# Two unused tiles that move the operands of the MoE matmuls to multiples of 512 bytes

## The chip, the cores and the metric

The kernel runs on one core of a Trainium2 chip. The metric is the device time of one execution in microseconds (us), as the median of three runs. Differences of about 0.2% are the least that a measurement of this kernel can tell from no change.

## What is computed

The reference chains three parts. The first is a retention-style attention over 4 batches, 8 heads, 576 positions and 64 features per head: scores are multiplied by a decay matrix (no softmax) and by the values. The second and third are feed-forward layers on the 2304 resulting tokens of 512 features: one with 2048 hidden units and a squared ReLU, and one with four experts of 1024 hidden units each, weighted by given probabilities.

```python
ret = scale * (q @ k.T) * Dmat            # Dmat[i, j] = gamma ** (i - j) for i >= j
x = (ret @ v) as [2304, 512]
x = square(relu(x @ w_in)) @ w_out        # 512 -> 2048 -> 512
p = probs / probs.sum(-1)
out = sum over e of p[:, e] * (relu(x @ w1[e]) @ w2[e])   # 4 x (512 -> 1024 -> 512)
```

## The kernel before, in words

**Numbers in two parts.** Each operand of a feed-forward matmul is kept as a pair of fp32r tiles, a rounded high part and the rest: `xh` and `xl` for tokens, `whi` and `wlo` for weights, `ghi` and `glo` for the hidden layer. A product is made of three matmuls: high by high, low by high, high by low.

**Stages.** The attention comes first, in its own pools, which are closed at its end; `finish` (L281) writes its result to `xh` and `xl`. Then comes what is called the MoE part here: a loop over 24 weight chunks c (8 of the first feed-forward layer, then 4 for each of the 4 experts), each of 256 hidden units (f = 0, 1 of 128 each), and inside it over five token groups g of 512, 512, 512, 512 and 256 tokens. For each (c, g), `layer1` (L356) runs, and after it the second layer of the pair before, `layer2_1` (L381) for c < 8 and `layer2_2` (L405) for c >= 8.

**Matmuls.** TensorE executes a matmul as a weight load of the stationary operand (128 columns here) and a stream of the moving operand.
- L365, `layer1`: stationary a slice of `whi` or `wlo`, moving a slice of `xh` or `xl`; 12 for each of two PSUM tiles.
- L389, `layer2_1`: stationary a slice of `whi` or `wlo`, moving `ghi` or `glo`; 6 for each of four PSUM tiles.
- L418, `layer2_2`: the other way round, stationary a slice of `ghi` or `glo`, moving a half of `whi` or `wlo`; 6 for each of g's 128-token blocks.

In all there are 4800 matmuls that stream 512 columns (2304 at L365, 768 at L389, 1728 at L418) and 768 that stream 256 (576 and 192, of the fifth group).

**Other engines.** ScalarE and VectorE empty the PSUM tiles (L369 to L376, L395 to L401, L424 to L428), GpSimd makes low parts (L122, L372, L401), and `split_w` (L101) converts the next chunk's weights while this one is used. The order on each engine is the order of the program.

**Where tiles lie.** Pools take space in each partition in the order in which they are opened, and a tile's size is rounded up to 32 bytes. The first free byte is 16512. `const` (L35) holds no tile in the kernel before. In the compiled program of before the tiles that MoE matmuls read begin at these bytes:

```
tile        bytes      begins at                 over a multiple of 512
xh, xl      36864      16512, 53376              128, 128
whi (2)      8192      123008, 131200            128, 128
wlo (2)      8192      139392, 147584            128, 128
pr, prsum   288, 72    192640, 192928            (not read by matmuls)
ghi (3)      4096      193024, 197120, 201216    0, 0, 0
glo (3)      4096      205312, 209408, 213504    0, 0, 0
```

All slices of them that a matmul reads begin a multiple of 512 bytes after the tile's start (128 columns of fp32r are 512 bytes, 512 columns 2048, a row of `xh` 9216), so each slice stands over a multiple of 512 as its tile does.

Of the kernel before, what the change touches and what calls it, by code (L numbers as in the profile page):

```python
# [6 lines left out]
F32 = mybir.dt.float32  # L7
# [25 lines left out]
def tile_kernel(ctx, tc, qT, kT, kn, vn, v4d, mask, qdec, kdec, wd, w, probs, out):  # L33
    nc = tc.nc
    const = ctx.enter_context(tc.tile_pool(name="const", bufs=1))  # L35
    xp = ctx.enter_context(tc.tile_pool(name="xp", bufs=1))
    wrp = ctx.enter_context(tc.tile_pool(name="wrp", bufs=4))
    cvp = ctx.enter_context(tc.tile_pool(name="cvp", bufs=1))
# [297 lines left out]
    with tc.manual_schedule():  # L336
# [4 lines left out]
        yp = ctx.enter_context(tc.tile_pool(name="yp", bufs=1))  # L341
# [3 lines left out]
        yacc = [yp.tile([128, KT, GS[g]], F32, name=f"y{g}", tag=f"acc{g}") for g in range(NG)]  # L345
        pr = yp.tile([128, NTT, 4], F32, name="pr")
        psum_ = yp.tile([128, NTT], F32, name="prsum")
        nc.sync.dma_start(out=pr, in_=probs)
        nc.vector.tensor_reduce(out=psum_, in_=pr, axis=mybir.AxisListType.X, op=ALU.add)
        nc.vector.tensor_scalar_add(psum_, psum_, 1e-9)  # L350
# [157 lines left out]
```

## Time and profile before

| | us |
|---|---|
| median of 3 runs | 1288.08 (1287.55 to 1289.81) |
| the profiled execution, its own time | 1288.76 |
| its span, first to last instruction | 1286.5 |
| PE (matmul) busy | 1272.8, 99% |
| PEld (weight load) busy | 1059.2, 82% |
| VectorE, GpSimd, ScalarE busy | 658.7, 332.9, 299.0 |

PE is TensorE's matmul stream, PEld its weight loads, which run beside it. The profile's duration of a matmul reaches into the next one, since matmuls are pipelined; what a matmul costs in a dense stream is the distance from its start to the next one's, called its pitch here. A row of the timeline gives the start in us, the duration, engine, line, and the tile written and the tiles read, the moving operand's high or low part and the stationary one's in the order of the profile's own names. A row of a group gives the number of instructions, their summed busy time in us, the mean of one in ns and the idle time before them.

### The profile page before, as it was taken

How to read it: one execution, taken by the hardware profiler on the slowest of the kernel's cores; microseconds unless marked ns; L12 is line 12 of the kernel's file. 1: busy time of each engine (PE TensorE's matmuls, PEld its weight loads, DVE VectorE, ACT ScalarE, POOL GpSimd, SP SyncE). 2: the span in 40 equal slices, each digit the busy share in tenths (PEclk: the TensorE clock that was granted, in tenths of full speed). 3: DMA queues.
4: the chain of work that ended last, by engine and by line, in shares of the span. 5: the costliest groups of instructions: out<-in, count | busy, mean ns of one | idle time of the engine just before them, and what ended most of it. 6: DMA issues, size and time to landing. Idle time of an engine off the chain costs nothing.

```text
span 1286.5 us, 16159 instructions
## 1 busy us (share of the span) xinstructions
PE 1272.8 (99%) x6720; PEld 1059.2 (82%) x6720; DVE 658.7 (51%) x946; ACT 299.0 (23%) x636; POOL 332.9 (26%) x270
## 2 busy tenths in 40 slices
PE   7999999999999999999999999999999999999998
PEld 6878888888888888888888888888888888888887
DVE  4965777887877851143343433434434433434334
ACT  3544322223222253311111111111111111111110
POOL 4654454444444592011010010110110110110100
PEclk9999999999999999999999999999999999999999
DMA  9931110111110000000000000000000000000003
GB/s 330 327 105 34 38 61 23 44 50 33 49 47 28 25 33 25 9 33 24 10 33 11 22 33 9 25 29 12 25 25 9 34 25 9 33 17 17 1 34 114
DMA packets 27465, 59.42 MB, mean 46 GB/s; under 512 B 3328, under 2 KB 4352, under 8 KB 27392
## 3 DMA queue, kind: packets, MB, share of 16 engines
q1 hardware_dynamic: 26880, 57.69, 13.1%
q8 instruction: 52, 0.85, 0.3%
q10 hardware_dynamic: 512, 0.70, 0.2%
q14 instruction: 21, 0.17, 0.0%
HBM read 53.66 MB, written 4.72 MB: 45 GB/s over the span
## 4 chain that ended last, share of the span: by engine, by line
PE 97%; DVE 1%; DMA 1%; ACT 0%; issue 0%; ACTq 0%; DVEq 0%
PE h L365 46%; PE o L418 31%; PE o L389 16%; PE xo L264 1%; PE qk L212 1%; PE xo L276 1%; PE state L240 1%; DMA v_n<-vn 1%; DMA k_n<-kn 0%; DVE cv_e L82 0%; DVE cv_p L86 0%; DVE xl L290 0%; ACT xh L289 0%; DVE pt L228 0%; DVE cv_m L88 0%; DVE cv_e L84 0%
## 5 line engine op out<-in xcount | busy, mean ns | idle before, releaser
L365 PE MATMUL h<-xh,whi 128*128 128x512 f32 (+1 forms) x960 | 353.7, 368 | 0.8 <-DVE xl L290 0.8
L365 PE MATMUL h<-xh,wlo 128*128 128x512 f32 (+1 forms) x960 | 354.2, 369 | 0.0
L365 PE MATMUL h<-xl,whi 128*128 128x512 f32 (+1 forms) x960 | 353.3, 368 | 0.0
L375 DVE SCALAR_TENSOR_TENSOR glo<-h,ghi 128x512 fp32r<-128x512 f32 (+1 forms) x160 | 102.2, 638 | 354.7 <-ACT ghi L374 354.7
L426 DVE SCALAR_TENSOR_TENSOR oacc<-o,pr,oacc 128x512 f32<-128x512 f32 x270 | 202.6, 750 | 139.4 <-PE o L418 135.1
L122 POOL TENSOR_TENSOR wlo<-wraw,whi 128x512 fp32r<-128x512 f32 x64 | 82.7, 1293 | 645.7 <-ACT whi L121 616.5
L374 ACT ACTIVATE ghi<-h 128x512 fp32r<-128x512 f32 (+1 forms) x160 | 89.0, 556 | 644.0 <-PE h L365 644.0
L418 PE MATMUL o<-whi,ghi 128*128 128x512 f32 x576 | 227.8, 395 | 0.0
L418 PE MATMUL o<-wlo,ghi 128*128 128x512 f32 x576 | 227.4, 395 | 0.0
L418 PE MATMUL o<-whi,glo 128*128 128x512 f32 x576 | 227.3, 395 | 0.0
L365 PEld LDWEIGHTS h<-xh,whi 128*128 128x128 f32 x960 | 180.8, 188 | 32.7 <-DVE xl L290 1.0
L365 PEld LDWEIGHTS h<-xl,whi 128*128 128x128 f32 x960 | 180.7, 188 | 32.2
L365 PEld LDWEIGHTS h<-xh,wlo 128*128 128x128 f32 x960 | 180.7, 188 | 30.9
L372 POOL TENSOR_TENSOR glo<-r,ghi 128x512 fp32r<-128x512 f32 (+1 forms) x80 | 95.8, 1199 | 142.6 <-ACT ghi L371 142.6
L370 DVE TENSOR_TENSOR r<-r 128x512 f32<-128x512 f32 (+1 forms) x80 | 81.4, 1017 | 94.9 <-ACT r L369 94.9
L418 PEld LDWEIGHTS o<-wlo,ghi 128*128 128x128 f32 x576 | 108.5, 188 | 25.7
L418 PEld LDWEIGHTS o<-whi,glo 128*128 128x128 f32 x576 | 108.7, 189 | 24.6
L418 PEld LDWEIGHTS o<-whi,ghi 128*128 128x128 f32 x576 | 108.5, 188 | 24.3
L389 PE MATMUL o<-ghi,wlo 128*128 128x512 f32 (+1 forms) x320 | 119.4, 373 | 0.0
L389 PE MATMUL o<-glo,whi 128*128 128x512 f32 (+1 forms) x320 | 119.1, 372 | 0.0
L389 PE MATMUL o<-ghi,whi 128*128 128x512 f32 (+1 forms) x320 | 119.0, 372 | 0.0
L397 DVE TENSOR_TENSOR y<-o,y 128x512 f32<-128x512 f32 (+1 forms) x140 | 85.5, 627 | 8.1 <-PE o L389 7.4
(51 smaller groups left out, 937.6 us busy)
## 6 DMA issues: line engine op xcount, KB each, us to landing
wraw<-wd SPq DMA_DIRECT2D x32, 512.0 KB, 3.6
wraw<-w SPq DMA_DIRECT2D x64, 256.0 KB, 2.7
q_t<-qT SPq DMA_DIRECT2D x16, 288.0 KB, 5.2
out<-oacc SPq DMA_DIRECT2D x18, 256.0 KB, 2.0
kt<-kT SPq DMA_DIRECT2D x15, 288.0 KB, 5.4
v_n<-vn SPq DMA_DIRECT2D x16, 256.0 KB, 4.8
k_n<-kn SPq DMA_DIRECT2D x15, 256.0 KB, 5.4
qd<-qdec SPq DMA_DIRECT2D x4, 224.0 KB, 5.0
```

Of the source, the lines that this page charges most:

```text
L122: nc.gpsimd.tensor_tensor(out=lo[:, s], in0=r, in1=f32(hi[:, s]), op=ALU.subtract)
L212: nc.tensor.matmul(qk[:, j, w : w + m], k_t[p, o : o + C], q_t[p, o : o + m], start=True, stop=True, skip_group_check=True,)
L240: nc.tensor.matmul(st[64 * j : 64 * j + 64, :], k_n[:, c, j, :], v_n[:, c, j, :], start=(c == 0), stop=(c == 3), skip_group_check=True,)
L365: nc.tensor.matmul(h, a[:, f, k, :], x[:, k, :], start=(n == 0), stop=(n == 3 * KT - 1))
L370: nc.vector.tensor_tensor(out=r, in0=r, in1=r, op=ALU.mult)
L372: nc.gpsimd.tensor_tensor(out=lo[:, f, :], in0=r, in1=f32(hi[:, f, :]), op=ALU.subtract)
L374: nc.scalar.activation(out=hi[:, f, :], in_=h, func=ACTF.Relu)
L375: nc.vector.scalar_tensor_tensor(out=lo[:, f, :], in0=h, scalar=0.0, in1=f32(hi[:, f, :]), op0=ALU.max, op1=ALU.subtract)
L389: nc.tensor.matmul(o, a[:, f, 128 * m : 128 * m + 128], x[:, f, :], start=(n == 0), stop=(n == 3 * FT - 1))
L397: nc.vector.tensor_tensor(out=y, in0=o, in1=y, op=ALU.add)
L418: nc.tensor.matmul(o, a[:, f, 128 * m : 128 * m + 128], x[:, f, :], start=(n == 0), stop=(n == 3 * FT - 1))
L426: nc.vector.scalar_tensor_tensor(out=acc, in0=o, scalar=pr[:, tt, e : e + 1], in1=acc, op0=ALU.mult, op1=ALU.add)
```

## The change

Two tiles are asked for and never written or read.

```diff
     const = ctx.enter_context(tc.tile_pool(name="const", bufs=1))
+
+    const.tile([128, 480], F32, name="pad0")
     xp = ctx.enter_context(tc.tile_pool(name="xp", bufs=1))
...
         psum_ = yp.tile([128, NTT], F32, name="prsum")
+        yp.tile([128, 32], F32, name="pad1")
         nc.sync.dma_start(out=pr, in_=probs)
```

`pad0` is 1920 bytes in each partition ahead of all other pools, and `pad1` is 128 bytes in `yp`, ahead of the pools of `ghi`, `glo` and `r`. By the sizes above, every tile from `xh` on begins 1920 bytes later, and `ghi`, `glo` and `r` 2048 bytes later: `xh` at 18432, `xl` at 55296, `whi` at 124928 and 133120, `wlo` at 141312 and 149504, the first `ghi` at 195072, the first `glo` at 207360. All of these are multiples of 512. The attention's tiles all move by the same 1920 bytes. No instruction is added, removed or reordered.

## Rows read from the trace of the kernel before

**Rows 1.** The profile's page, busy time of PE, and granted clock in 40 slices.
```profile
PE 1272.8 (99%) x6720; PEld 1059.2 (82%) x6720; DVE 658.7 (51%) x946; ACT 299.0 (23%) x636; POOL 332.9 (26%) x270
...
PEclk9999999999999999999999999999999999999999
```

**Rows 2.** The page's chain that ended last, by engine and by line.
```profile
PE 97%; DVE 1%; DMA 1%; ACT 0%; issue 0%; ACTq 0%; DVEq 0%
PE h L365 46%; PE o L418 31%; PE o L389 16%; PE xo L264 1%; PE qk L212 1%; PE xo L276 1%; PE state L240 1%; DMA v_n<-vn 1%; DMA k_n<-kn 0%; DVE cv_e L82 0%; DVE cv_p L86 0%; DVE xl L290 0%; ACT xh L289 0%; DVE pt L228 0%; DVE cv_m L88 0%; DVE cv_e L84 0%
```

**Rows 3.** Busy time by stage: stretch, its us, engines' busy (count), clock, DMA.
```profile
0.00:85.00 85.00, 74.91 (x1153) 65.35 (x1153) 59.79 (x96) 40.08 (x166) 47.97 (x50) 1.00 0.83 288
85.00:480.00 395.00, 395.00 (x1888) 329.97 (x1889) 291.22 (x414) 123.55 (x225) 199.52 (x153) 1.00 0.12 38
480.00:1283.00 803.00, 802.85 (x3681) 663.90 (x3680) 307.03 (x437) 135.33 (x245) 85.41 (x68) 1.00 0.07 24
```

**Rows 4.** Timeline of PE: the MoE part's first and last matmul.
```profile
84.91 0.50 PE L365 MATMUL h<-xh,whi 128*128 128x512 f32 x1 [0.84 <-DVE xl L290]
...
1282.46 0.40 PE L418 MATMUL o<-wlo,ghi 128*128 128x512 f32 x1
```

**Rows 5.** Groups of matmuls by line and shape, whole span, one row of three.
```profile
L365 PE MATMUL h<-xh,wlo 128*128 128x512 f32 x768 | 300.0, 391 | 0.0
...
L418 PE MATMUL o<-whi,ghi 128*128 128x512 f32 x576 | 227.8, 395 | 0.0
...
L389 PE MATMUL o<-ghi,wlo 128*128 128x512 f32 x256 | 101.2, 395 | 0.0
...
L365 PE MATMUL h<-xh,wlo 128*128 128x256 f32 x192 | 54.2, 282 | 0.0
```

**Rows 6.** Timeline, PE and PEld, second half of an L365 block, then L389.
```profile
215.27 0.39 PE L365 MATMUL h<-xh,whi 128*128 128x512 f32 x1
...
217.76 0.39 PE L365 MATMUL h<-xh,wlo 128*128 128x512 f32 x1
217.77 0.19 PEld L389 LDWEIGHTS o<-ghi,whi 128*128 128x128 f32 x1
217.99 0.40 PE L389 MATMUL o<-ghi,whi 128*128 128x512 f32 x1
...
223.58 0.28 PE L365 MATMUL h<-xh,whi 128*128 128x256 f32 x1
```

**Rows 7.** Timeline, PE and PEld, one L365 block and the L418 block behind it.
```profile
700.84 0.39 PE L365 MATMUL h<-xh,whi 128*128 128x512 f32 x1
...
706.07 0.40 PE L365 MATMUL h<-xh,wlo 128*128 128x512 f32 x1
706.07 0.19 PEld L418 LDWEIGHTS o<-whi,ghi 128*128 128x128 f32 x1
...
706.30 0.40 PE L418 MATMUL o<-whi,ghi 128*128 128x512 f32 x1
...
711.65 0.40 PE L418 MATMUL o<-wlo,ghi 128*128 128x512 f32 x1
711.89 0.39 PE L365 MATMUL h<-xh,whi 128*128 128x512 f32 x1
```

**Rows 8.** Group of one: the last L365 matmul ahead of L389 (at 217.76).
```profile
L365 PE MATMUL h<-xh,wlo 128*128 128x512 f32 x1 | 0.4, 389 | 0.0
```

**Rows 9.** Group of one: the last L365 matmul ahead of L418 (at 706.07).
```profile
L365 PE MATMUL h<-xh,wlo 128*128 128x512 f32 x1 | 0.4, 396 | 0.0
```

**Rows 10.** Timeline of PE: twelve 256-column matmuls, then L418.
```profile
724.35 0.28 PE L365 MATMUL h<-xh,whi 128*128 128x256 f32 x1
...
725.79 0.39 PE L418 MATMUL o<-whi,ghi 128*128 128x512 f32 x1
```

**Rows 11.** Groups of VectorE and GpSimd that follow each PSUM tile.
```profile
L426 DVE SCALAR_TENSOR_TENSOR oacc<-o,pr,oacc 128x512 f32<-128x512 f32 x270 | 202.6, 750 | 139.4 <-PE o L418 135.1
...
L372 POOL TENSOR_TENSOR glo<-r,ghi 128x512 fp32r<-128x512 f32 (+1 forms) x80 | 95.8, 1199 | 142.6 <-ACT ghi L371 142.6
```

## The prediction

> **What bounds the kernel now.** I read the page's first lines, then the chain of work that ended last, then busy time by stage. [...] By stage, the attention takes the first 85 us; from there to 1283 us PE has no gap worth naming (395.00 busy of 395, 802.85 of 803) [rows 3]. So nothing that waits, loads or copies can give time back in the MoE part. Only the pitch of the matmuls can.
>
> The MoE part runs from 84.91 to 1282.46 us plus its last matmul's pitch of 0.23 [rows 4], 1197.8 us in all, for 4800 matmuls of 512 columns and 768 of 256.
>
> **The pitch is not one number.** In the rows by shape a 512-column matmul has a mean duration of 391 ns at L365 (390 in its two rows that are not shown) but 395 ns at L418 and at L389 (394 in one row not shown) [rows 5]. The durations reach into the next matmul, so I take pitches from the timeline. The second half of an L365 block goes from 215.27 to 217.99, twelve matmuls in 2.72 us: 226.7 ns each. The L389 block behind it goes from 217.99 to 223.58, 24 matmuls in 5.59 us: 232.9 ns [rows 6]. An L418 block goes from 706.30 to 711.89, again 24 in 5.59: 232.9 ns [rows 7]. Duration less pitch is 162 ns in both cases (389 less 226.7, 395 less 232.9) [rows 5, 6, 8], so differences of mean durations are differences of pitch.
>
> Three things could tell the slow lines from the fast one: the length of the group that shares a PSUM tile (6 against 12), the code, and the addresses. The border between blocks separates them. While a matmul streams, PEld loads the stationary operand of the next one: both start within 0.01 us [rows 6, 7]. The last L365 matmul ahead of an L389 block streams `xh` (128 bytes over a multiple of 512) beside a load of `whi` (also 128): 389 ns [rows 8]. The same instruction ahead of an L418 block streams `xh` (128) beside a load of `ghi` (0): 396 ns [rows 9]. It is the same line, group length, position and moving tile; only the operand that is loaded meanwhile differs. So I take it that the pair read at one time sets the pitch: both at the same distance from a multiple of 512 is fast, 128 bytes apart is slow. L389 streams 0 beside loads of 128, L418 streams 128 beside loads of 0, and both show 232.9. Multiples of 512 beyond that don't count: L365 reads weight slices at eight of them, and the second half of the block at 215.27 keeps 226.7 through four.
>
> One border doesn't fit at once: the last L418 matmul, at 711.65, streams `whi`'s twin `wlo` (128) beside a load of `whi` (128), and its pitch is still 0.24 [rows 7]. And an L365 block behind an L418 block takes 5.46 us, 227.5 ns each (700.84 to 706.30), against 226.7 in a settled half [rows 6, 7]. I read both as time to settle after a slow block: L365's mean of 390.3 (391, 390 and 390 in its three rows) lies 1.3 above the 389 of a settled one [rows 5, 8]. After the change no pair differs, so nothing is left to settle from.
>
> **The change part by part.**
>
> *pad0* moves the attention, `xh`, `xl`, `whi` and `wlo` by 1920 bytes, which is 384 over a multiple of 512; *pad1* moves `ghi` and `glo` by 128 more. No instruction, semaphore or DMA is added, and an unused tile has no reader to wait for. What it costs is space: the highest tile, the third `r`, ends 2048 bytes higher. Afterwards all MoE operands stand at 0 over a multiple of 512, so each pair is equal, as at L365 now.
>
> - L418: 1728 matmuls from 395 to 389 ns: 1728 x 6 = 10.4 us less [rows 5, 8].
> - L389: 768 of 512 columns from 394.7 (mean of the three rows) to 389: 4.4 us less.
> - L365: 2304 of 512 columns from 390.3 (mean of the three) to 389: 3.0 us less.
> - 256 columns: twelve from 724.35 to 725.79 are 120.0 ns each in a settled half [rows 10], and the mean of 282 less 162 is 120 too [rows 5]. Nothing here.
>
> Sum: 10.4 + 4.4 + 3.0 = 17.8 us. The other way round, free of the rounding of means to 1 ns: 4800 x 0.2267 + 768 x 0.120 = 1180.3 us in place of 1197.8 [rows 4, 6, 10], 17.5 less. I take 17.5.
>
> All of it is on the path, as PE is what ends the stage. What would be late next is far off: VectorE's step for an L418 tile takes 750 ns where the tile's six matmuls will take 1360, with 135 us idle in wait for PE, and GpSimd's 1199 ns at L372 stands beside twelve matmuls of 2720 ns [rows 11].
>
> *The attention* moves as a whole, so no distance between two of its tiles changes. Its 85 us have loads and engines interleaved (PE 74.91 of 85 busy) [rows 3]. If distance alone counts it costs nothing. The trace has no row at the new positions; the nearest price is 7 ns (396 less 389) [rows 8, 9] for each of its 1152 matmuls either way, 8 us if all were bound by their streams. I take 0, since their starts hang on other engines too, and keep 1 us either way for the range.
>
> [...]
>
> **The rivals.**
>
> *No change.* The two sorts of matmul differ for another reason that goes with the tile (its place in the partition, or that it was written shortly before), and moving all by a few hundred bytes alters nothing; or the unused tiles take no space. For it: the border shows which tile, not which address bit. Against it: `ghi` and `glo` lie in six places over 24 KB and `whi` and `wlo` in four, and L389 and L418 swap their roles at the same pitch [rows 6, 7]. Time 1288.
>
> *Slower: an operand at a multiple of 512 is what costs.* The slow pairs are just those with one operand at 0; the fast ones have none. No pair of the trace has both at 0, and after the change every one has. If it costs 6 ns for each such operand, L365 pays 2 x 6 above 389 (10.7 above its mean; 2304 x 10.7 = 24.7 us) and the 2496 others 6 more than now (15.0): 1288.1 + 39.7 = 1328. If the second costs nothing, only L365 loses, 4.7 x 2304 = 10.8: 1299. It decides from the first L365 block on. [...]
>
> *More than forecast: the constant goes too.* From 256 to 512 columns the settled pitch grows by 106.7 ns (226.7 less 120.0) [rows 6, 10], that is 2.4 columns a ns; so both carry a constant of 13.3 ns. If that were a matter of position too, 5568 x 13.3 = 74 us more would go: 1196.5. Against it: it is the same at both widths and at every slice. [...]
>
> *Half.* L389 or L418 settles at a pitch of its own between the two: 8 us less, 1280.
>
> **How the numbers follow.** Forecast 0.70: 1288.1 - 17.5 = 1270.6, within 2 us either way. The profiled execution, 1288.76 for a span of 1286.5, should come to a span near 1269.0, and its time lies 0.7 above the median. Half 0.06, no change 0.11, slower 0.09, more 0.04. The range must take in no change to leave out less than 2 in 10: 1267 to 1290, which holds 0.87. A measurement tells about 0.2%, 2.6 us, from no change: faster 0.80 (forecast, half, more), same 0.11, slower 0.09.
>
> **What would show it.** Right: mean durations of 389 ns in all nine 512-column groups; blocks of 24 at L389 and L418 in 5.44 us; no settling at the start of an L365 block. Wrong: 395 at L418 and L389 as before (no change); L365 above 391 (slower); anything under 385 (more). The prediction falls if the position of each operand counts for itself and not the distance of the two.

## The result

The changed kernel takes 1271.7 us (median of four runs, 1271.3 to 1272.47) against 1288.6 us for the kernel before, run beside it: a ratio of 0.987, 95% interval 0.985 to 0.989. The forecast was 1270.6 us. The profiled execution has a span of 1269.1 us (forecast 1269.0) and a time of 1271.3.

The page of the changed kernel, busy time and the chain that ended last. TensorE is as full as before and the chain lies where it did [rows 1, 2], and its granted clock is 1.00 in both stages, as the rows by stage below show.

```profile
PE 1254.8 (99%) x6720; PEld 1057.3 (83%) x6720; DVE 650.4 (51%) x946; ACT 298.7 (24%) x636; POOL 334.2 (26%) x270
...
PEclk9999999999999999999999999999999999999999
...
PE 97%; DVE 2%; DMA 0%; ACT 0%; issue 0%; ACTq 0%; DVEq 0%
```

Matmuls of the changed kernel by line and shape (L368, L421 and L392 are L365, L418 and L389 of before; columns as in [rows 5]).

```profile
L368 PE MATMUL h<-xh,whi 128*128 128x512 f32 x768 | 299.0, 389 | 0.8 <-DVE xl L292 0.8
...
L368 PE MATMUL h<-xh,wlo 128*128 128x512 f32 x768 | 298.8, 389 | 0.0
L421 PE MATMUL o<-whi,ghi 128*128 128x512 f32 x576 | 224.3, 389 | 0.0
...
L421 PE MATMUL o<-wlo,ghi 128*128 128x512 f32 x576 | 224.1, 389 | 0.0
L392 PE MATMUL o<-ghi,whi 128*128 128x512 f32 x256 | 99.7, 389 | 0.0
...
L392 PE MATMUL o<-ghi,wlo 128*128 128x512 f32 x256 | 99.6, 389 | 0.0
L368 PE MATMUL h<-xh,wlo 128*128 128x256 f32 x192 | 54.3, 283 | 0.0
```

All nine groups of 512 columns stand at 389 ns, where the kernel before had 394 to 395 at L418 and L389 and 390 to 391 at L365 [rows 5]. The groups of 256 columns moved by 1 ns at most.

Timeline of PE in the changed kernel: one L392 block (start to start, 24 matmuls), and the first half of the next one, which follows matmuls of 256 columns.

```profile
215.77 0.39 PE L392 MATMUL o<-ghi,whi 128*128 128x512 f32 x1
...
221.21 0.28 PE L368 MATMUL h<-xh,whi 128*128 128x256 f32 x1
...
224.08 0.40 PE L392 MATMUL o<-ghi,whi 128*128 128x512 f32 x1
...
226.83 0.39 PE L392 MATMUL o<-ghi,whi 128*128 128x512 f32 x1
```

The first block takes 5.44 us, 226.7 ns for each matmul, where its like took 5.59 before [rows 6]. The first half of the next takes 2.75 us for twelve, 229.2 ns each: behind 256-column matmuls there is still a short settling.

Busy time by stage of the changed kernel (columns as in [rows 3]), cut at the MoE part's first matmul and behind its last one.

```profile
0.00:84.36 84.36, 73.67 (x1152) 64.42 (x1153) 60.02 (x96) 40.00 (x166) 48.66 (x50) 1.00 0.83 290
84.36:1265.29 1180.93, 1180.93 (x5568) 992.87 (x5568) 589.65 (x849) 258.72 (x470) 285.56 (x220) 1.00 0.09 29
```

The MoE part takes 1180.9 us in place of 1197.8, 16.9 less. It starts 0.55 earlier [rows 4], which is the rest of the 17.4 by which the span fell; the tail behind it is 3.8 us in both.

### The profile page after: what moved, and what is told of

Same layout as the page of the kernel before. It is cut to its first block, busy times and chain, and to the rows that moved or that the text cites. A ratio compares the mean times of both kernels' runs of the same rounds, so it can differ in the third digit from the quotient of the medians.

```text
span 1269.1 us, 16159 instructions
## 1 busy us (share of the span) xinstructions
PE 1254.8 (99%) x6720; PEld 1057.3 (83%) x6720; DVE 650.4 (51%) x946; ACT 298.7 (24%) x636; POOL 334.2 (26%) x270
## 4 chain that ended last, share of the span: by engine, by line
PE 97%; DVE 2%; DMA 0%; ACT 0%; issue 0%; ACTq 0%; DVEq 0%
PE h L368 47%; PE o L421 31%; PE o L392 16%; PE xo L266 1%; PE qk L214 1%; PE xo L278 1%; PE state L242 1%; DMA k_n<-kn 0%; DVE cv_e L84 0%; DVE xl L292 0%; DVE cv_e L86 0%; DVE pt L230 0%; ACT xh L291 0%; DVE pt L228 0%; DVE cv_e L82 0%
## 5 line engine op out<-in xcount | busy, mean ns | idle before, releaser
L368 PE MATMUL h<-xh,whi 128*128 128x512 f32 (+1 forms) x960 | 353.2, 368 | 0.8 <-DVE xl L292 0.8
L368 PE MATMUL h<-xl,whi 128*128 128x512 f32 (+1 forms) x960 | 353.2, 368 | 0.0
L368 PE MATMUL h<-xh,wlo 128*128 128x512 f32 (+1 forms) x960 | 353.1, 368 | 0.0
L421 PE MATMUL o<-whi,ghi 128*128 128x512 f32 x576 | 224.3, 389 | 0.0
L421 PE MATMUL o<-whi,glo 128*128 128x512 f32 x576 | 224.3, 389 | 0.0
L421 PE MATMUL o<-wlo,ghi 128*128 128x512 f32 x576 | 224.1, 389 | 0.0
L368 PEld LDWEIGHTS h<-xh,whi 128*128 128x128 f32 x960 | 181.0, 189 | 31.7 <-DVE xl L292 1.0
L368 PEld LDWEIGHTS h<-xl,whi 128*128 128x128 f32 x960 | 180.9, 188 | 30.5
L368 PEld LDWEIGHTS h<-xh,wlo 128*128 128x128 f32 x960 | 180.9, 188 | 30.0
L373 DVE TENSOR_TENSOR r<-r 128x512 f32<-128x512 f32 (+1 forms) x80 | 78.4, 981 | 95.8 <-ACT r L372 95.8
L421 PEld LDWEIGHTS o<-wlo,ghi 128*128 128x128 f32 x576 | 108.1, 188 | 22.6
L421 PEld LDWEIGHTS o<-whi,ghi 128*128 128x128 f32 x576 | 108.2, 188 | 22.1
L421 PEld LDWEIGHTS o<-whi,glo 128*128 128x128 f32 x576 | 108.2, 188 | 21.8
L392 PE MATMUL o<-glo,whi 128*128 128x512 f32 (+1 forms) x320 | 117.8, 368 | 0.0
L392 PE MATMUL o<-ghi,whi 128*128 128x512 f32 (+1 forms) x320 | 117.8, 368 | 0.0
L392 PE MATMUL o<-ghi,wlo 128*128 128x512 f32 (+1 forms) x320 | 117.7, 368 | 0.0
```

The source lines that it names most:

```text
L368: nc.tensor.matmul(h, a[:, f, k, :], x[:, k, :], start=(n == 0), stop=(n == 3 * KT - 1))
L373: nc.vector.tensor_tensor(out=r, in0=r, in1=r, op=ALU.mult)
L392: nc.tensor.matmul(o, a[:, f, 128 * m : 128 * m + 128], x[:, f, :], start=(n == 0), stop=(n == 3 * FT - 1))
L421: nc.tensor.matmul(o, a[:, f, 128 * m : 128 * m + 128], x[:, f, :], start=(n == 0), stop=(n == 3 * FT - 1))
```

## The experiments

Every experiment starts from the kernel before and only moves tiles, so the same instructions run on the same numbers. "Place" is a tile's start over a multiple of 512 bytes, the "load" is that of a matmul's stationary operand, and the "stream" is its moving operand. A time without a range is that of one execution, and the time in brackets behind it is the kernel before on the same chip. The lines added move L365, L389 and L418 down by one to three.

### Each unused tile alone

```diff
         psum_ = yp.tile([128, NTT], F32, name="prsum")
+        yp.tile([128, 32], F32, name="pad1")
```

> Only pad1 is added: xh, xl, whi, wlo stay 128 bytes over a multiple of 512, and ghi, glo go from 0 to 128. Distance theory (only the distance of the two operands read at one time counts): all pairs equal, every 512-column group at 389 ns, time as of the changed kernel, 1271.7 within 2 us. Position theory (an operand gains by standing at a multiple of 512): no operand stands there any more, so no gain, 1288 or more. Attention unmoved, so it stays at the 84.9 us of before.

Measured: 1271.7 us (1271.1 to 1272.2) against 1289.3, ratio 0.986, interval 0.985 to 0.988. By line and shape:

```profile
L366 PE MATMUL h<-xh,whi 128*128 128x512 f32 x768 | 299.0, 389 | 0.8 <-DVE xl L290 0.8
...
L419 PE MATMUL o<-whi,ghi 128*128 128x512 f32 x576 | 224.3, 389 | 0.0
...
L390 PE MATMUL o<-ghi,whi 128*128 128x512 f32 x256 | 99.7, 389 | 0.0
```

The same busy times to 0.1 us as in the changed kernel, with no operand at a multiple of 512. 128 bytes in one place are the whole gain.

```diff
     const = ctx.enter_context(tc.tile_pool(name="const", bufs=1))
+    const.tile([128, 480], F32, name="pad0")
```

> Only pad0 is added: xh, xl, whi, wlo at 0, ghi and glo at 384 over a multiple of 512, so the pairs of L365 are equal as before and those of L389 and L418 are still 128 bytes apart (384 against 0). Distance theory: as before, L389 and L418 at 395 ns, 1288 within 2 us, less up to 0.6 us for the attention. Position theory: L365 and half the operands of the other two stand at multiples of 512, so some part of the gain, 1276 to 1283.

Measured: 1288.5 us (before: 1289.3). By line and shape:

```profile
L366 PE MATMUL h<-xh,wlo 128*128 128x512 f32 x768 | 300.0, 391 | 0.0
...
L419 PE MATMUL o<-whi,ghi 128*128 128x512 f32 x576 | 227.8, 395 | 0.0
...
L390 PE MATMUL o<-ghi,wlo 128*128 128x512 f32 x256 | 101.2, 395 | 0.0
```

Each of these three rows equals that of before to the tenth of a microsecond [rows 5]. A shift of all tiles alike does nothing to the MoE part, although it puts `xh`, `xl`, `whi` and `wlo` at multiples of 512.

### Equal places that are a multiple of nothing larger than 32

```diff
+    const.tile([128, 8], F32, name="pad0")
...
+        yp.tile([128, 32], F32, name="pad1")
```

> A pad of 32 bytes ahead of all tiles and one of 128 ahead of ghi and glo: all operands at 160 over a multiple of 512, equal, but at no multiple of 64. Distance theory: 389 ns in every 512-column group, 1271.5 within 2 us. If equal operands must also stand at a multiple of 64 or 128 bytes: above 389 ns in all three lines, 1275 or more.

Measured: 1271.3 us (before: 1290.2), all nine groups of 512 columns at 389 ns. So the single operand needs no alignment beyond 32 bytes here.

### The lines change places

```diff
+    wpad = ctx.enter_context(tc.tile_pool(name="wpad", bufs=1))
+    wpad.tile([128, 32], F32, name="padw")
     wp = ctx.enter_context(tc.tile_pool(name="wp", bufs=2))
...
+        yp.tile([128, 32], F32, name="pad1")
```

> 128 bytes are put ahead of whi and wlo, and 128 more ahead of ghi and glo: xh, xl at 128, all the others at 256. The pairs of L365 are now 128 apart, those of L389 and L418 equal. Distance theory: the lines change places, L365 at 395 ns, L389 and L418 at 389 to 390; 2304 x (232.9 less 227.9) = 11.5 us more and 2496 x 5.9 = 14.8 less, 1285. Theory that an operand at 0 is what costs, or that lines of six matmuls in a group are slow for themselves: L365 stays at 389 to 390; 1271 by the first (no operand at 0), 1288 by the second.

Measured: 1287.2 us (before: 1289.3). By line and shape:

```profile
L368 PE MATMUL h<-xh,wlo 128*128 128x512 f32 x768 | 303.4, 395 | 0.0
L368 PE MATMUL h<-xh,whi 128*128 128x512 f32 x768 | 303.2, 395 | 0.8 <-DVE xl L292 0.8
...
L421 PE MATMUL o<-wlo,ghi 128*128 128x512 f32 x576 | 224.7, 390 | 0.0
...
L392 PE MATMUL o<-ghi,wlo 128*128 128x512 f32 x256 | 100.0, 391 | 0.0
```

The line that was fast is slow, and the two slow ones are fast. It is neither the six matmuls of a group, nor the code, nor the region in which `ghi` and `glo` lie, nor an operand at a multiple of 512 (there is none here). The time came out 2 us above the expected 1285: L418 and L389 stay at 389 to 391, as L365 did in the kernel before, so not all of their 6 ns came back.

### How far apart

Only the size of the pad ahead of `ghi` and `glo` changes: 40, 48, 56, 80 or 96 columns of 4 bytes, so that these two lie 32, 64, 96, 192 or 256 bytes from the other tiles' place.

```diff
+        yp.tile([128, 96], F32, name="pad1")
```

> Only a pad of 384 bytes ahead of ghi and glo: they stand at 384, the rest at 128, 256 bytes apart. If the distance counts modulo 256 (128 and 384 apart gave the same pitch in the kernel before): equal in effect, L389 and L418 at 389 ns, 1272. If it counts modulo 512: slow pairs, L389 and L418 at 393 to 401 ns, 1283 to 1303.

> Only ghi and glo move, to 192 over a multiple of 512, the rest at 128: 64 bytes apart. If any distance that is no multiple of 256 bytes is equally slow: L389 and L418 at 395 ns, 1288. If what counts is how near the distance is to 128: between, 391 to 393 ns, 1277 to 1283. If distances below 128 are free: 389 ns, 1272. A pitch under 226.7 ns (386 ns or less) would mean that equal positions are not the best choice.

> As before, with ghi and glo 32 bytes apart from the rest (160 and 128). If any distance is equally slow: 395 ns, 1288. If graded: 389 to 391 ns, 1272 to 1277. If free below 128: 389 ns, 1272.

> As before, with ghi and glo 96 bytes apart from the rest (224 and 128). If any distance is equally slow: 395 ns, 1288. If graded by nearness to 128: 393 to 395 ns, 1282 to 1288. If free below 128: 389 ns, 1272.

> Only ghi and glo move, to 320 over a multiple of 512, 192 bytes from the rest, which is 64 the other way modulo 256. With 64 apart L389 (stream ahead of the load by 64) had a pitch of 229.6 and L418 (stream behind by 64) 233.3. If only the distance modulo 256 with its sign counts, the lines change places: L389 at 395 to 396 ns, L418 at 391 to 392, and 1728 x 3.7 - 768 x 3.7 = 3.6 us less than with 64: 1284.5. If the line counts and not the sign: as with 64, 1288.

Measured, with mean durations over the three groups of a line (L389 and L418 by their names in the kernel before):

| bytes apart | L389, ns | L418, ns | us | before, us |
|---|---|---|---|---|
| 0 (`pad1` alone) | 389 | 389 | 1271.7 | 1289.3 |
| 32 | 395 | 395 | 1287.7 | 1290.2 |
| 64 | 392 | 396 | 1288.1 | 1290.2 |
| 96 | 395 | 396 | 1293.9 | 1290.2 |
| 128 (kernel before) | 395 | 395 | 1288.6 | |
| 192 | 394 | 391 | 1280.4 | 1289.1 |
| 256 | 389 | 389 | 1271.1 | 1289.3 |

256 bytes apart is as good as 0: 389 ns on both lines, 1271.1 us and 1271.7. So among these runs the distance counts modulo 256. Within 256 it is neither graded by nearness to 128 nor equally bad everywhere. 32 is as bad as 128 (395 ns on both lines), and 64 is milder on one side only (392 at L389, 396 at L418). By line and shape, with 64 bytes between the places:

```profile
L419 PE MATMUL o<-whi,glo 128*128 128x512 f32 x576 | 227.8, 396 | 0.0
...
L390 PE MATMUL o<-ghi,whi 128*128 128x512 f32 x256 | 100.8, 394 | 0.0
L390 PE MATMUL o<-ghi,wlo 128*128 128x512 f32 x256 | 100.2, 391 | 0.0
L390 PE MATMUL o<-glo,whi 128*128 128x512 f32 x256 | 100.0, 390 | 0.0
```

The same view with 192 bytes between them:

```profile
L419 PE MATMUL o<-whi,glo 128*128 128x512 f32 x576 | 226.7, 394 | 0.0
L419 PE MATMUL o<-whi,ghi 128*128 128x512 f32 x576 | 225.3, 391 | 0.0
L419 PE MATMUL o<-wlo,ghi 128*128 128x512 f32 x576 | 224.3, 389 | 0.0
...
L390 PE MATMUL o<-ghi,wlo 128*128 128x512 f32 x256 | 100.9, 394 | 0.0
```

With 64 the stream of L389 stands 64 above the load, and that of L418 64 below. With 192, which is 64 the other way modulo 256, the two lines change places: the milder case is the stream 64 above the load, on either line (392 ns at L389 with 64, 391 at L418 with 192). The time at 192 is 4 us below the expected 1284.5: by the starts in the traces of 64 and 192, 1.9 of these are L365, which the expectation left out, 1.2 are L418, and 1.0 is an attention that ended earlier than with 64 (84.85 us against 85.90). In the milder case the three groups of a line differ, from 389 to 394, although their operands stand at the same distance: what tells these groups apart isn't shown. No distance gave a 512-column group below 389.

The 1293.9 us at 96 are 5 above the kernel before. Two of these are the attention, none of whose tiles moved: the MoE part began at 86.86 us in place of 84.91, and the granted clock of the first 84 us was 0.98, where the kernel before has 1.00 (columns as in [rows 3]).

```profile
0.00:84.00 84.00, 73.40 (x1118) 64.17 (x1120) 57.35 (x94) 38.93 (x162) 48.13 (x50) 0.98 0.86 291
```

The other 3 lie in the MoE part, at a clock of 1.00: from start to start L418 has 233.9 ns there and L389 233.7, about 1 ns more than at 128 bytes.

### Which of two loads counts

The prediction held that a stream meets the load of the next matmul's stationary operand. `wlo` alone 128 bytes off the rest, which has equal places:

```diff
     wp = ctx.enter_context(tc.tile_pool(name="wp", bufs=2))
+    wpad = ctx.enter_context(tc.tile_pool(name="wpad", bufs=1))
+    wpad.tile([128, 32], F32, name="padw")
+    wpl = ctx.enter_context(tc.tile_pool(name="wpl", bufs=2))
...
-        lo = wp.tile([128, WC], F32R, name="wlo")
+        lo = wpl.tile([128, WC], F32R, name="wlo")
```

> wlo alone is moved 128 bytes from the others: xh, xl, whi, ghi, glo at 128 over a multiple of 512, wlo at 256. Each group of three matmuls at L365 and L389 has one that uses wlo as its stationary operand and one that streams while wlo is loaded. If the pair read at the same time counts (a stream beside the load of the next stationary operand): at L365 the group h<-xl,whi and at L389 o<-glo,whi, both ahead of the wlo matmul, are the long ones, 393 ns or more, the others 389 to 391. If the matmul's own pair counts: h<-xh,wlo and o<-ghi,wlo are the long ones. At L418 both theories name o<-wlo,ghi. Time, with a third of the 4800 pairs apart at about 6 ns: 1271.7 + 1600 x 6 ns = 1281, between 1275 and 1288, since a slow matmul also delays or speeds up its neighbours.

Measured: 1289.7 us (before: 1289.1), by line and shape:

```profile
L368 PE MATMUL h<-xh,wlo 128*128 128x512 f32 x768 | 304.8, 397 | 0.0
L368 PE MATMUL h<-xl,whi 128*128 128x512 f32 x768 | 304.0, 396 | 0.0
L368 PE MATMUL h<-xh,whi 128*128 128x512 f32 x768 | 299.0, 389 | 0.8 <-DVE xl L293 0.8
L421 PE MATMUL o<-wlo,ghi 128*128 128x512 f32 x576 | 227.5, 395 | 0.0
L421 PE MATMUL o<-whi,glo 128*128 128x512 f32 x576 | 225.2, 391 | 0.0
L421 PE MATMUL o<-whi,ghi 128*128 128x512 f32 x576 | 224.1, 389 | 0.0
```

Both theories fell as they were put: at L365 two of three are long, the stream beside the load of `wlo` (396) and the matmul that uses `wlo` (397). At L418 `o<-wlo,ghi` is long, as both said, but `o<-whi,glo` ahead of it also has 391, with every operand that it meets at an equal place. A third of the pairs of stream and next load apart cost the whole gain; the time is 9 us above the expected 1281 and outside the range that was given with it. That a slow matmul also delays or speeds up its neighbours, the reason put beside that range, was the author's estimate; this run doesn't separate such an effect from the pairing. Two readings were left: a matmul is long if its stream is apart from its own stationary operand or from the next one, or one bad load makes two matmuls long. `xl` alone 128 bytes off (modulo 256) tells them apart, as there one matmul meets both:

```diff
+    xp.tile([128, 32], F32, name="padx")
     xl_ = xp.tile([128, KT, NT], F32R, name="xl")
+    xp.tile([128, 32], F32, name="pady")
...
+        yp.tile([128, 32], F32, name="pad1")
```

> xl alone is moved 128 bytes from the others (modulo 256): xh, whi, wlo, ghi, glo at 128 or 384 over a multiple of 512, xl at 256. At L365 the matmul h<-xl,whi then streams apart from its own stationary whi and apart from wlo, which is loaded meanwhile; all other pairs are equal. If a matmul is long where its stream is apart from its own stationary operand or from the next one (which fits all groups of lo_apart): h<-xl,whi at 395 to 397 ns, h<-xh,wlo and h<-xh,whi at 389 to 390, L389 and L418 at 389, time 1271.7 + 768 x 7 ns = 1277. If only the load of the next one counts and makes two matmuls long, its neighbour and the one that uses it (the other reading of lo_apart): h<-xh,wlo long as well, 397, time 1271.7 + 768 x 13.2 ns = 1282.

Measured: 1275.6 us (before: 1288.5), by line and shape:

```profile
L368 PE MATMUL h<-xl,whi 128*128 128x512 f32 x768 | 303.1, 395 | 0.0
L368 PE MATMUL h<-xh,whi 128*128 128x512 f32 x768 | 299.3, 390 | 0.8 <-DVE xl L292 0.8
L368 PE MATMUL h<-xh,wlo 128*128 128x512 f32 x768 | 298.5, 389 | 0.0
```

Only the stream of `xl` is long, and the matmul behind it, whose `wlo` was loaded beside that stream, is not. So of the two it is the first reading: the stream has to agree with its own stationary operand and with the next one, and a disagreement with both costs once (395 ns for 389 to 390). It leaves the 391 of `o<-whi,glo` above without a cause. The time is 1.4 us below the expectation; 1.2 of that are the first layer's 256-column matmuls, which have 280 to 282 ns here and 282 to 283 with `pad1` alone.

## Why the prediction was right

- **What bounds, and what can give time back.** Right: the stage without gaps became shorter by the pitch of its matmuls and by nothing else; PE is busy for all of its 1180.93 us.
- **Distance, not position.** Shown by four runs: `pad0` alone leaves every row of the MoE part as it was, `pad1` alone gives all, places of 160 serve as well as 0, and with `whi` and `wlo` moved the fast line turns slow. The title's multiples of 512 are one of several ways to equal places (128 and 160 gave 389 ns too).
- **The terms.** By summed durations L418 lost 9.8 us (682.5 to 672.7 over its three groups), L389 4.2 and L365 2.2, where 10.4, 4.4 and 3.0 were forecast; the stage's own difference is 16.9 of 17.5. The small shortfall has the step "nothing is left to settle from" behind it. A block behind 256-column matmuls still starts at 229.2 ns, with every place equal. By the starts in the trace this is so all 32 times that 512 columns follow 256, at eight L365 blocks too, for which the prediction named "no settling" as a sign. The first five 512-column matmuls of these blocks lose 0.9 us together against 226.7 ns each, and the first 256-column ones of their blocks give 0.2 back, which is the 0.6 that the MoE part fell short. So the change of width disturbs as well, and L365's 1.3 ns above its settled value were not all due to the borders of unequal places.
- **The attention at 0.** The 0.55 us that it lost are within its own scatter: with the attention unmoved the MoE part began at 84.7 us (`pad1` alone) and at 84.1 (256 apart), and with all of it moved at 84.7 (`pad0` alone). That the span agreed with the forecast to 0.1 us was luck: this came on top of a MoE part that fell 0.6 short.
- **The border that didn't fit.** The prediction read the pitch of 0.24 at 711.65 [rows 7] as settling. The last two experiments give a better cause: that matmul streams `wlo` (128) over its own stationary `ghi` (0), and its own operand counts as well. The step "only the operand that is loaded meanwhile" was half of the rule. It cost no accuracy here, because after the change both halves are satisfied at once.
- **The rivals.** No change would have needed a cause that goes with the tile's region or line; the run in which the lines change places excludes it. Slower needed a price for operands at multiples of 512; in the kernel with `pad0` alone L365 reads both its operands there, and keeps 391 in its row. More needed the constant of 13.3 ns to go. For 512 columns it stayed at every place tried, as no group fell below 389; 256-column matmuls did fall below their 283, to 279 at 32 bytes. Half didn't occur with equal places; a distance of 192 bytes looks like it, at 1280.4 us.

## What to carry to other kernels

Where fp32r matmuls of 512 columns follow one another without gaps, compare their mean durations by line: a difference of some ns at equal shapes (395 for 389 here) can be a matter of which operands are paired, and the starts of the tiles modulo 256 bytes are the first thing to look at. Put all operands of such a stream, moving and stationary, at the same place modulo 256; which place did not matter here (0, 128 and 160 over a multiple of 512 were equally fast), and one small unused tile ahead of the pool that is off (128 bytes here) does it. Small tiles in a pool ahead of the operands (288 and 72 bytes) were what upset it unseen.

## What the runs showed of the hardware

- A dense stream of fp32r matmuls, each with its own load of 128 columns, has, with all places equal, a settled pitch of 226.7 ns for 512 columns and 120.0 for 256 in the changed kernel. A line through these two gives 2.4 columns a ns and a constant of 13.3 ns.
- The places of stream and load count together: with 32, 64, 96, 128 or 192 bytes between them a 512-column matmul had 391 to 396 ns on the average of a line, and 389 with 0 or 256: 2 to 7 ns more, 6 at 128 bytes.
- Both neighbours count: the stationary operand in use (397 ns with `wlo` alone off) and the one loaded for the next matmul (396 there, 389 with equal places). Why the one in use does, although its load, 0.19 us from 217.77 on, has been shown as ended when the stream begins at 217.99 [rows 6], no row tells.
- The loss isn't symmetric: a stream 64 bytes above the load loses 2 to 3 ns on average (391 and 392 for 389), one 64 bytes below it 5 to 7 (394 and 396). What lies behind the period of 256 bytes isn't shown by any run here.
- No loss above 1 ns shows in the groups of 256 columns that meet unequal places (284 ns at most, for 282 to 283). With 32 bytes between the places those of L389 are even shorter, 279 ns. One group in the kernel before, and the same one with 32 bytes:

```profile
L389 PE MATMUL o<-ghi,wlo 128*128 128x256 f32 x64 | 18.2, 284 | 0.0
```

```profile
L390 PE MATMUL o<-ghi,wlo 128*128 128x256 f32 x64 | 17.8, 279 | 0.0
```
